# Batch 0's keys in float32 on two hardware queues, with the units of batches 1 to 4 placed anew

## The chip, the cores and the metric

The kernel runs on one core of one Trainium2 chip. The metric is the device time in microseconds (us); three runs of the kernel before gave a median of 245.89 us.

A core has five engines that run beside each other, each through its own instructions in order: TensorE (PE, matrix products), VectorE (DVE), ScalarE (ACT), GpSimd (POOL) and SyncE (SP). Transfers between main memory and on-chip memory (DMA) are issued from SP's, ACT's or POOL's queue. In the profile SP's queue is q1, ACT's is q10 (both "hardware_dynamic") and POOL's is q0 ("software_dynamic").

## What is computed

```python
a = softmax(phi, axis=2)                      # over the sequence; phi is [b, h, s, 32]
k_m = einsum('bhsm,bhsd->bhmd', a, k)         # 32 memory keys a head
v_m = einsum('bhsm,bhsd->bhmd', a, v)         # 32 memory values a head
attn = softmax(q @ k_m.T / sqrt(64), axis=-1)
x = (attn @ v_m)                              # [b, h, s, d] -> [b*s, h*d]
out = ((x @ w_a) * (x @ w_b)) @ w_out
```

There are 8 batches, 8 heads, 576 tokens and a head size of 64, so x has 4608 rows of 512. w_a and w_b are 512 x 1536, w_out is 1536 x 512. All inputs and the output are float32; the kernel computes in float16 with float32 sums.

## The kernel before, in words

The kernel never forms x. For each batch it computes the memory keys and values, folds the values into w_a and w_b (the tile vab), and multiplies vab with the attention weights (the tile A). The products are called "up"; their product by elements goes to the tile ht, and the product of ht with w_out is called "down".

**Units.** The work of a batch ahead of its ups is cut into small pieces (units(b)), which are named by short strings:

- exp0, exp1: exp of half of phi, on ACT (line 194). Phi of batch 0 comes by one DMA, so both wait for all of it.
- ks0, ks1 and vs0, vs1: PE sums of exp times keys and times values, for head groups 0 and 1 (L255), each followed by DVE instructions. ks0 needs keys 0:2, ks1 keys 2:4. For batches 2 and up, kv (L212) does all sums and km (L227, L232, tile rep) takes them to on-chip memory on DVE.
- kt0, kt1, vt0, vt1, or kvt for later batches: PE transposes of those sums, and a DVE copy into kvT (L276, L242).
- qt0 to qt3: DVE transposes of a quarter of q (L203).
- s0, s1 or sc: scores on PE (L292), with four PSUM banks for sc; e0, e1: their exp on ACT (L305).
- den0, den1: sums of E on PE (L314), and the logarithm on ACT (L315).
- nr0, nr1: exp of the negative logarithm on ACT (tile R, L323), and A = E x R (L325), on DVE for batches 0 and 1 and on POOL after.
- v0, v1, v2: PE products that fold a third of w_a and w_b (tile pva, L337); x0a, x0b and so on: the copies to vab, one on ACT and one on DVE (L349). hv and hx are the same for halves of the first third.
- L: load(b + 2), four DMAs on POOL's queue. A number in y3 or y11 means so many down products of the first four row blocks (L389): y1 to y16 need the first third of w_out, y17 to y32 the second, and the rest the last.

A prime in the strings means the batch after, an underscore the batch before.

**Order.** The order is written out by hand. chain(0, ...) and chain(1, ...) run the units of batches 0 and 1 in the order of a string, with f4 for four products of a tile of zeros that keep PE busy. From batch 1 on, ups(...) runs half-steps: four up products (L592), their copy on ACT (a_sb, L600) and the product by elements on DVE (ht, L603); then some of the down products that are due (class Work, L464) and then the next slot of a string. A slot holds units joined by "+"; "-" is empty. The string `second` is used in batch 2 and holds the units of batch 3 and, with a prime, the first ones of batch 4; `every` comes after. The downs of later blocks work on pairs of row blocks with sums of ht (h_sums, L446) that POOL prepares; they are emitted when Work pulls a product that is near them.

**PSUM.** There are eight banks. Banks.take gives the one that was not taken or freed for longest and isn't held, so a product can wait for the ACT or DVE copy that empties its bank.

**Start.** Phi of batch 0 goes by SP's queue and the first half of its keys by ACT's, both in float32. The keys wait in the space of ht and a DVE instruction casts them (L156). The second half of the keys, q, v, the weights and all later batches go by POOL's queue, which casts to float16 on the way (phi stays float32). After the casts DVE fills the tile ones (L160), which two POOL instructions (L161, L163) then change before POOL issues the second third of w_a. 28 fill products run on PE before ks0.

Of the kernel before, what the change touches and what calls it, by code (L numbers as in the profile page):

```python
# [8 lines left out]
F32 = mybir.dt.float32  # L9
# [9 lines left out]
def kernel(  # L19
# [11 lines left out]
    nc = tc.nc  # L31
# [38 lines left out]
    def rows(x, b):  # L70
        return x[b].rearrange("h s d -> (h s d)").rearrange("(c p f) -> p c f", c=NHP, p=P)

    phis, qs, kvs = {}, {}, {}
    kv_sbs = [consts.tile([P, 3, NHP, NI * D], F16, name=f"kv_sb{t}") for t in range(2)]

    def load_phi(b):
        phis[b] = inp.tile([P, NHP, NI * M], F32, name="phi_sb")
        (nc.sync if b == 0 else nc.gpsimd).dma_start(out=phis[b], in_=rows(phi, b))

    def load_k(b, hps=slice(0, NHP)):  # L80
        kvs[b] = kv_sbs[b % 2]
        nc.gpsimd.dma_start(out=kvs[b][:, 0, hps], in_=rows(k, b)[:, hps])

    def load_v(b, hps=slice(0, NHP)):
        nc.gpsimd.dma_start(out=kvs[b][:, 1, hps], in_=rows(v, b)[:, hps])

    def load_q(b, hps=slice(0, NHP)):
        if b not in qs:
            qs[b] = inp.tile([P, NHP, NI * D], F16, name="q_sb")
        nc.gpsimd.dma_start(out=qs[b][:, hps], in_=rows(q, b)[:, hps])  # L90

    def load(b):
        load_phi(b)
        load_k(b)
        load_v(b)
        load_q(b)

    def load_wab(lo, hi):
        nc.gpsimd.dma_start(out=wa_sb[:, :, lo:hi], in_=wa_rows[:, :, lo:hi])
        nc.gpsimd.dma_start(out=wb_sb[:, :, lo:hi], in_=wb_rows[:, :, lo:hi])  # L100
# [4 lines left out]


    ht = consts.tile([P, NFF, 2 * S], F16, name="ht")
    k_f32 = ht[:, 0:2].bitcast(F32)
    nc.scalar.dma_start(out=k_f32, in_=rows(k, 0)[:, 0:2])
    nc.scalar.preload_act_table_set("natural_log_exp_and_others")  # L110
    load_phi(0)
    halves = [slice(0, 2), slice(2, 4)]
    load_q(0, halves[0])
    load_k(0, halves[1])
    load_q(0, halves[1])
    load_v(0)
    kvs[0] = kv_sbs[0]

    warm = consts.tile([P, 512], F16, name="warm")
    nc.vector.memset(warm, 0.0)  # L120
# [26 lines left out]
    def fill(n, cols=512):  # L147

        pw = banks.tile([P, 512], F32, name="pw")
        for _ in range(n):  # L150
            nc.tensor.matmul(pw[:, :cols], warm[:, :P], warm[:, :cols], start=True, stop=True)
# [1 line left out]
    ident = consts.tile([P, P], F16, name="ident")  # L153
    make_identity(nc, ident)
    nc.vector.memset(kv_sbs[0][:, 2], 1.0 / CS)
    nc.vector.tensor_copy(out=kvs[0][:, 0, 0:2], in_=k_f32)  # L156
    load_wab(0, 512)

    ones = consts.tile([P, 4, 32], F16, name="ones")
# [429 lines left out]
    def up_half(b, i, hf, x):  # L589
        ps = banks.tile([P, HALF], F32, name=("pa", "pb")[x])  # L590
        for g in range(2):
            nc.tensor.matmul(ps, vabs[b][x][:, g, P * i:P * (i + 1)], attn[b][:, g, HALF * hf:HALF * (hf + 1)],  # L592
                             start=(g == 0), stop=(g == 1))
        if x == 0:
            if b == 0:
                n = (2 * i + hf) % 20
                a_sbs[b, i, hf] = spare[:, HALF * n:HALF * (n + 1)]
            else:
                a_sbs[b, i, hf] = apool.tile([P, HALF], F16, name="a_sb")
            nc.scalar.copy(out=a_sbs[b, i, hf], in_=ps)  # L600
        else:
            t0 = S * (b % 2) + HALF * hf
            nc.vector.tensor_tensor(out=ht[:, i, t0:t0 + HALF], in0=a_sbs.pop((b, i, hf)), in1=ps, op=ALU.mult)  # L603

    def up(b, i, hfs):
        for hf in hfs:
            up_half(b, i, hf, 0)
        if len(hfs) > 1:
            yield
        for hf in hfs:  # L610
            up_half(b, i, hf, 1)
        yield

    def ups(steps, side=()):

        side = iter(side)
        for step in steps:
            for _ in up(*step):
                work.advance()
                next(side, us[step[0]]["-"])()  # L620
        for f in side:
            work.advance()
            f()
# [5 lines left out]
    def half_steps(b, hf, lo=0):  # L629

        return [(b, i, (hf,)) for i in range(lo, NFF)]
# [10 lines left out]
    def slots(b, names):  # L642

        def both(fs):
            return lambda: [f() for f in fs]
        def unit(n):
            if n == "fin":
                return lambda: work.pull(-work.done % NFF)
            if n == "L":
                return lambda: load(b + 2) if b + 2 < B else None  # L650
            if n[0] == "y":
                return lambda: some(int(n[1:]))
            if n[0] == "d" and n[1:].isdigit():
                return lambda: work.pull(int(n[1:]))
            return us[b + n.endswith("'") - n.endswith("_")][n.rstrip("'_")]

        return [both([unit(n) for n in x.split("+")]) for x in names.split()]
# [3 lines left out]
    def some(n):  # L661
        for _ in range(n):
            next(early, None)

    def chain(b, plan):


        for x in plan.split():
            if x[0] == "f":
                fill(int(x[1:]), 256)  # L670
            elif x[0] == "y":
                some(int(x[1:]))
            elif x[0] in "ab":
                i, _, hf = x[1:].partition(".")
                for h in ([int(hf)] if hf else (0, 1)):
                    up_half(b, int(i), h, "ab".index(x[0]))
            else:
                us[b][x]()
# [3 lines left out]
    chain(0, "v0a x0a f4 a0 a1 v0b x0b f4 b0 b1 a2 b2 v1a x1a a3 b3 a4 a5 v1b x1b a6 a7 b4 b5 v2a x2a b6 b7 a8 a9")  # L682
    load(2)
    chain(0, "v2b x2b a10 a11 b8 b9 b10 b11")
    chain(1, "exp0 exp1 y9 ks0 y3 kt0 qt0 qt1 y1 y3 ks1 qt2 s0 e0 y6 kt1 qt3 den0 y3 s1 nr0 e1 y4 y2 den1 vs0 vs1 vt0 y1 vt1 nr1 hv0a hx0a hv0b y3 hx0b y2")
    load(3)
    sum_weights()
    ups(steps(1, 0, 4), slots(1, "- hv1a+hx1a hv1b+hx1b+y1 - v1a+x1a y3+v1b x1b y3"))
    ups(half_steps(1, 0, 4), slots(1, "- v2a+x2a+v2b+x2b+qt0' - - qt1'+exp0'+qt2' exp1' - kv'+km'+y9"))
    work.plan(S + HALF, 10)  # L690
    ups(half_steps(1, 1, 4), slots(2, "- kvt qt3 sc+e0+e1 - den0+den1 nr0+nr1 v0+x0a x0b - v1+x1b x1a"))
    second = "v2_+x2a_+exp0 x2b_ exp1 - kv+km qt0 qt1 kvt qt2+qt3 sc+e0 e1+v0+x0a den0+x0b v1+x1a nr0+L x1b+exp0' den1 - nr1+v2+x2a - x2b+exp1' - kv'+km' qt0'+qt1' - qt2'+kvt'+qt3'"
    every = "- sc+e0 e1 den0 v0+x0a+x0b - - nr0+exp0' - - v1+x1a qt0' x1b+den1 exp1' - v2+x2a+x2b nr1+qt1' kv'+km' qt2' - qt3' - kvt'+L -"
    last = "sc+e0 - e1 - v0+x0b - x0a den1 - - den0 v1+x1b x1a+nr0 - - - - nr1+v2+x2a - - - - - x2b"
    for b in range(2, B):
# [37 lines left out]
```

The softmax here doesn't subtract the row's maximum and nothing guards it: scores larger than these inputs give would overflow.

## Time and profile before

| | |
|---|---|
| Median of 3 runs | 245.89 us (245.75 to 246.15) |
| The profiled execution | 245.71 us, span 244.0 us |
| Granted PE clock | 0.996 |
| PE, DVE, ACT, POOL busy | 234.6, 166.2, 157.2, 155.6 us |
| Phi of batch 0: issue, landing | 0.81, about 7.0 us |
| First half of batch 0's keys: issue, landing | 0.81, about 6.6 us |
| First key sums (ks0) on PE | 8.81 us |
| Landing of the second third of w_out | 41.06 us |
| First up product of batch 2 | 73.55 us |

The span runs from the first to the last instruction of the program. In the timeline a row is: start, busy time, engine, line, operation, tiles written and read, shapes, count, and in brackets how long the engine stood idle before it and what ended that. PE's matmuls overlap, so a stall can also hide in the length of a row: then the start times tell. POOLq, SPq and ACTq stand for the issue of a DMA.

### The profile page before, as it was taken

The page shows a single profiled execution, that of the slowest core. Times are in us where ns is not written, and L with a number is a line of the kernel's source. Part 1 is how long each engine was busy: PE and PEld are TensorE (multiplying, and loading weights), DVE is VectorE, ACT ScalarE, POOL GpSimd, SP SyncE. Part 2 cuts the span into 40 slices and gives each one's busy share as a digit, 9 for nine tenths or more (in the row PEclk, how much of TensorE's full clock was granted, in tenths as well). Part 3 has the DMA queues.
Part 4 walks back from the last instruction along what each step waited for, and adds up shares of the span by engine and source line. Part 5 has one row for each costly group of instructions (what it writes and reads, how often), then busy time and mean ns, then how long its engine had stood idle before and what let it go on. Part 6 is the DMA issues. An engine that isn't in the chain of part 4 may idle for free.

```text
span 244.0 us, 7661 instructions
## 1 busy us (share of the span) xinstructions
PE 234.6 (96%) x3043; PEld 168.1 (69%) x3043; DVE 166.2 (68%) x401; ACT 157.2 (64%) x406; POOL 155.6 (64%) x130
## 2 busy tenths in 40 slices
PE   7989998999989999999999999999999999999993
PEld 2555654456757857767788777877787878888882
DVE  3446773568949968875994659865996676756642
ACT  2265761679598589578956768587856867565330
POOL 8722263499879629892889759892849177937001
PEclk9999999999999999999999999999999999999998
DMA  6999999999937955973159732696120403042154
GB/s 198 211 207 206 209 254 208 254 224 280 224 89 167 205 110 121 236 128 81 41 146 205 177 86 46 166 203 152 34 58 3 89 0 87 3 89 61 42 128 118
DMA packets 25044, 33.82 MB, mean 139 GB/s; under 512 B 1936, under 2 KB 19472, under 8 KB 25008
## 3 DMA queue, kind: packets, MB, share of 16 engines
q0 software_dynamic: 18288, 22.84, 50.8%
q1 hardware_dynamic: 6208, 9.70, 15.8%
q10 hardware_dynamic: 512, 0.79, 1.0%
q8 instruction: 24, 0.39, 0.7%
q14 instruction: 12, 0.10, 0.1%
HBM read 42.47 MB, written 9.44 MB: 213 GB/s over the span
## 4 chain that ended last, share of the span: by engine, by line
PE 76%; DMA 16%; DVE 3%; ACT 2%; issue 1%; POOL 0%; DVEq 0%
PE pa L592 17%; PE py L464 17%; PE pb L592 16%; PE pv L464 8%; DMA wo_sb<-in_moe_w_out_dram 7%; DMA wa_sb<-in_moe_w_a_dram 6%; PE pva L337 5%; PE px L464 4%; PE po L389 3%; DMA ht<-in_k_dram 2%; PE pkv L212 2%; PE pscore L292 1%; PE pD L314 1%; PE pT L241 1%; ACT E L305 1%
## 5 line engine op out<-in xcount | busy, mean ns | idle before, releaser
L603 DVE TENSOR_TENSOR ht<-a_sb,pb 128x288 f16<-128x288 f16 x168 | 73.2, 448 | 39.4 <-ACT a_sb L600 29.9
L592 PEld LDWEIGHTS <-vab 128*128 128x128 f16 x768 | 71.6, 98 | 27.1 <-issue 9.4
L600 ACT CAST a_sb<-pa 128x288 f16<-128x288 f32 x168 | 66.6, 407 | 26.4 <-PE pa L592 24.3
L592 PE MATMUL pa<-A,vab 128*128 128x288 f16 x384 | 75.7, 287 | 0.4 <-DVE vab L349 0.2
L592 PE MATMUL pb<-A,vab 128*128 128x288 f16 x384 | 75.0, 286 | 0.3 <-ACT vab L349 0.3
L446 POOL TENSOR_TENSOR h_sums<-ht 128x768 f16<-128x768 f16 x28 | 45.9, 1642 | 33.0 <-DVE ht L603 32.4
L464 PEld LDWEIGHTS <-h_sums 128*128 128x128 f16 x384 | 37.3, 98 | 7.0 <-issue 0.5
L349 DVE CAST vab<-pva 128x512 f16<-128x512 f32 (+1 forms) x50 | 32.3, 663 | 3.3 <-PE pva L337 2.6
L349 ACT CAST vab<-pva 128x512 f16<-128x512 f32 (+1 forms) x50 | 27.9, 581 | 9.3 <-PE pva L337 9.1
L464 PEld LDWEIGHTS <-ht 128*128 128x128 f16 x288 | 28.1, 98 | 5.7 <-issue 0.4
L464 PE MATMUL py<-w_sums,h_sums 128*128 128x256 f16 x192 | 30.4, 272 | 0.0
L446 POOL TENSOR_TENSOR h_sums<-ht,h_sums 128x768 f16<-128x768 f16 x14 | 23.0, 1642 | 1.0
L446 POOL TENSOR_TENSOR h_sums<-h_sums,ht 128x768 f16<-128x768 f16 x14 | 23.0, 1642 | 0.9
L325 POOL TENSOR_TENSOR A<-E,R 128x576 f16<-128x576 f16 x12 | 15.3, 1278 | 8.8 <-ACT R L323 8.6
L305 ACT ACTIVATE E<-pscore 128x288 f16<-128x288 f32 x32 | 11.4, 417 | 14.5 <-PE pscore L292 14.5
L464 PE MATMUL pv<-w_sums,h_sums 128*128 128x256 f16 x96 | 16.2, 273 | 0.0
L464 PE MATMUL py<-wo_sb,ht 128*128 128x256 f16 x96 | 16.0, 273 | 0.0
L471 ACT ACTIVATE u<-py 128x256 f32<-128x256 f32 x32 | 12.6, 393 | 5.2 <-PE py L464 4.9
L203 DVE STREAM_TRANSPOSE qT<-q_sb 128x288 f32<-128x288 f32 x32 | 14.3, 461 | 2.3 <-DMA q_sb<-in_q_dram 2.3
L464 PE MATMUL py<-w_sums,ht 128*128 128x256 f16 x96 | 15.5, 272 | 0.1
L464 PE MATMUL px<-wo_sb,ht 128*128 128x256 f16 x96 | 15.4, 273 | 0.0
L194 ACT ACTIVATE exp_sb<-phi_sb 128x576 f16<-128x576 f32 x16 | 11.0, 698 | 5.3 <-DMA phi_sb<-in_phi_dram 5.3
(65 smaller groups left out, 274.5 us busy)
## 6 DMA issues: line engine op xcount, KB each, us to landing
out_dram<-o_sb SPq DMA_DIRECT2D x68, 128.0 KB, 2.4
kv_sb<-in_v_dram POOLq DMA_DIRECT2D x7, 576.0 KB, 11.4
phi_sb<-in_phi_dram POOLq DMA_DIRECT2D x7, 576.0 KB, 5.2
kv_sb<-in_k_dram POOLq DMA_DIRECT2D x7, 576.0 KB, 9.0
q_sb<-in_q_dram POOLq DMA_DIRECT2D x6, 576.0 KB, 13.6
wa_sb<-in_moe_w_a_dram POOLq DMA_DIRECT2D x3, 512.0 KB, 14.4
wb_sb<-in_moe_w_b_dram POOLq DMA_DIRECT2D x3, 512.0 KB, 16.2
wo_sb<-in_moe_w_out_dram POOLq DMA_DIRECT2D x3, 512.0 KB, 18.1
```

The source lines that it names most:

```text
L194: nc.scalar.activation(out=t["exp"][:, 2 * z:2 * z + 2, :, :], in_=phis[b][:, 2 * z:2 * z + 2, :].rearrange("p c (i m) -> p c i m", m=M), ...
L203: nc.vector.transpose(out=t["qT"][:, hp, :].bitcast(F32), in_=qs[b][:, hp, :].bitcast(F32))
L305: nc.scalar.activation(out=Ev[:, g, :, z, :], in_=pss, func=AF.Exp, scale=1.0 / (8.0 * CS))
L325: engine.tensor_tensor(out=attn[b][:, g, sl], in0=t["E"][:, g, sl], in1=t["R", g][:, sl], op=ALU.mult)
L337: nc.tensor.matmul(t["pva", lo, z][g][0][32 * j:32 * j + 32, 0:hi - lo], t["kvT"][64 * r:64 * r + 64, 4 + g, M * j:M * j + M], w_sbs[z][64 ...
L349: engine_copy(out=vabs[b][z][:, g, lo:hi], in_=pva[:, 0:hi - lo])
L446: engine.tensor_tensor(out=out, in0=in0, in1=in1, op=op)
L464: nc.tensor.matmul(po, lhs[:, i], rhs[:, i], start=first and i == 0, stop=i == KH - 1, skip_group_check=not first)
L471: nc.scalar.mul(out=x, in_=po, mul=scale)
L592: nc.tensor.matmul(ps, vabs[b][x][:, g, P * i:P * (i + 1)], attn[b][:, g, HALF * hf:HALF * (hf + 1)], start=(g == 0), stop=(g == 1))
L600: nc.scalar.copy(out=a_sbs[b, i, hf], in_=ps)
L603: nc.vector.tensor_tensor(out=ht[:, i, t0:t0 + HALF], in0=a_sbs.pop((b, i, hf)), in1=ps, op=ALU.mult)
```

## The change

Five things are changed.

1. Both halves of batch 0's keys are loaded in float32, the first on SP's queue and the second on ACT's. The second half leaves POOL's queue.
2. Phi of batch 0 is issued on SP's queue behind the first key half.
3. DVE casts the two halves in two instructions, both ahead of the tile ones.
4. In chain(1) the units and the early downs have another order: twelve downs before ks0, ks1 directly behind it, kt1 before the six downs that need the second third of w_out, qt0 and qt1 apart, vs and vt spread.
5. In the slots of batch 2 (in the second half of batch 1) qt3 comes first, nr0 goes with den0 and den1, and nr1 one slot later. In `second`, kvt and nr0 of batch 3 come one slot earlier, den1 three slots later (the 19th), nr1 four later (the 22nd); of batch 4, exp1 comes three slots earlier, and qt0 and qt1 come in the 19th and 22nd slots instead of together in the 23rd.

```diff
-    k_f32 = ht[:, 0:2].bitcast(F32)
-    nc.scalar.dma_start(out=k_f32, in_=rows(k, 0)[:, 0:2])
+    k_f32 = ht[:, 0:4].bitcast(F32)
+    halves = [slice(0, 2), slice(2, 4)]
+    for engine, x in zip((nc.sync, nc.scalar), halves):
+        engine.dma_start(out=k_f32[:, x], in_=rows(k, 0)[:, x])
     nc.scalar.preload_act_table_set("natural_log_exp_and_others")
     load_phi(0)
-    halves = [slice(0, 2), slice(2, 4)]
-    load_q(0, halves[0])
-    load_k(0, halves[1])
-    load_q(0, halves[1])
+    kvs[0] = kv_sbs[0]
+    for x in halves:
+        load_q(0, x)
     load_v(0)
-    kvs[0] = kv_sbs[0]
...
-    nc.vector.tensor_copy(out=kvs[0][:, 0, 0:2], in_=k_f32)
+    for x in halves:
+        nc.vector.tensor_copy(out=kvs[0][:, 0, x], in_=k_f32[:, x])
...
-    chain(1, "exp0 exp1 y9 ks0 y3 kt0 qt0 qt1 y1 y3 ks1 qt2 s0 e0 y6 kt1 qt3 den0 y3 s1 nr0 e1 y4 y2 den1 vs0 vs1 vt0 y1 vt1 nr1 hv0a hx0a hv0b y3 hx0b y2")
+    chain(1, "exp0 y1 exp1 y11 ks0 ks1 y1 qt0 y3 kt0 qt1 s0 e0 kt1 y6 qt2 qt3 den0 y3 s1 nr0 y4 vs0 e1 vs1 den1 y1 vt1 y2 vt0 nr1 hv0a hx0a hv0b y2 hx0b y3")
...
-    ups(half_steps(1, 1, 4), slots(2, "- kvt qt3 sc+e0+e1 - den0+den1 nr0+nr1 v0+x0a x0b - v1+x1b x1a"))
-    second = "v2_+x2a_+exp0 x2b_ exp1 - kv+km qt0 qt1 kvt qt2+qt3 sc+e0 e1+v0+x0a den0+x0b v1+x1a nr0+L x1b+exp0' den1 - nr1+v2+x2a - x2b+exp1' - kv'+km' qt0'+qt1' - qt2'+kvt'+qt3'"
+    ups(half_steps(1, 1, 4), slots(2, "qt3 kvt - sc+e0+e1 - den0+den1+nr0 - v0+nr1+x0a x0b - v1+x1b x1a"))
+    second = "v2_+x2a_+exp0 x2b_ exp1 - kv+km qt0 kvt+qt1 - qt2+qt3 sc+e0 e1+v0+x0a den0+x0b nr0+v1+x1a L x1b+exp0' - exp1' v2+x2a den1+qt0' x2b - nr1+qt1'+kv'+km' - - qt2'+kvt'+qt3'"
```

## The prediction

> **What bounds the kernel now.** I read the page first, then the DMA queues in short windows, the chain of waits, and the timelines of each engine around every place where TensorE (PE) stops. Page, busy times and slices:
>
> ```profile
> span 244.0 us, 7661 instructions
> PE 234.6 (96%) x3043; PEld 168.1 (69%) x3043; DVE 166.2 (68%) x401; ACT 157.2 (64%) x406; POOL 155.6 (64%) x130
> ...
> DMA  6999999999937955973159732696120403042154
> ```
>
> PE is busy nearly all the time, so only its stalls and the warm-up fills can be won. DMA is full in the ten slices after the first (6 to 67 us). DMA queues in three windows (2 to 3, 4 to 5, 7 to 8 us; packets, MB written, share):
>
> ```profile
> q1 hardware_dynamic: 109, 0.13, 66.2%
> q10 hardware_dynamic: 11, 0.03, 14.7%
> ...
> q10 hardware_dynamic: 118, 0.27, 68.6%
> q1 hardware_dynamic: 118, 0.14, 37.6%
> ...
> q0 software_dynamic: 187, 0.20, 119.7%
> ```
>
> The casting queue q0 writes 0.20 MB a us in half precision, so it reads 0.41; the two hardware queues together moved 0.41 from 4 us on. Either way the core reads about 410 GB/s: a byte of float32 costs the same on each queue. Only 2 to 4 us is below it (151 and 271 GB/s). PE's timeline:
>
> ```profile
> 37.23 0.68 PE L255 MATMUL pk<-kv_sb,exp_sb 64*32 64x128 f16 x36 [0.80 <-DMA kv_sb<-in_k_dram]
> ...
> 41.10 1.45 PE L389 MATMUL po<-wo_sb,ht 128*128 128x512 f16 x6 [0.24 <-DMA wo_sb<-in_moe_w_out_dram]
> ...
> 85.65 0.47 PE L292 MATMUL pscore<-qT,kvT 32*32 32x288 f16 x32
> ...
> 103.54 1.15 PE L292 MATMUL pscore<-qT,kvT 32*32 32x288 f16 x32
> ```
>
> Until 41 us PE follows the loads (keys of batch 1, then the second third of w_out). The chain says the same: DMA 16%, and one step from w_out's issue at 22.95 to its landing at 41.06. Later stalls are short: the same 32 score matmuls take 0.47 us at 85.65 and 1.15 at 103.54. POOL's and ACT's timelines, for the steps that move:
>
> ```profile
> 89.11 1.64 POOL L446 TENSOR_TENSOR h_sums<-ht 128x768 f16<-128x768 f16 x1 [5.86 <-DVE ht L603]
> 91.58 1.28 POOL L325 TENSOR_TENSOR A<-E,R 128x576 f16<-128x576 f16 x1 [0.84 <-ACT R L323]
> ...
> 99.20 1.27 POOL L325 TENSOR_TENSOR A<-E,R 128x576 f16<-128x576 f16 x1
> 100.43 1.65 POOL L446 TENSOR_TENSOR h_sums<-ht 128x768 f16<-128x768 f16 x1
> ...
> 70.19 1.36 ACT L323 ACTIVATE R<-L 128x576 f16<-128x576 f32 x2
> ```
>
> **What the Trainium skill says.** DMA: Bandwidth & Descriptors, section "Issuing engines are not separate DMA queues": all issuers' transfers run on the same 16 engines, and more issuers save issue time alone. The trace agrees: 410 GB/s read on both kinds. Same page, "Queues, rings and completion order": each DMA engine takes the queues in turn by packets. Between 98 and 98.5 us q0 moved 45 packets and q1 35, which fits. Same page, "SWDGE vs HWDGE vs iDMA": a cast is possible only from GpSimd; so keys on the other queues stay float32, and VectorE (DVE) must cast them.
>
> **The change, part by part.**
>
> *Start, queues.* POOL loses one DMA issue (0.73 us at 2.18), so its later issues come 0.73 earlier; they only join a queue that is full. SP gains one issue (0.45) ahead of phi's. ACT issues the other half instead. DVE gains a second cast of 0.76; the casts are followed by the memset of ones and POOL's two selects (7.65 and 8.03), ahead of POOL's next weight issue. Keys should land at about 5.7 instead of 6.64, since they no longer share with phi; casts to 7.2, so that place does not move. If keys land as late as now, POOL's issue is 0.8 late, hidden by 9 us of loads already queued.
>
> Bytes: 0.59 MB leave q0 and come to hardware; at 410 GB/s both are 1.44 us, net nothing. What can be won is the slope at the start. At 2 to 3 us q1 moved 109 packets of 1152 bytes, each some 95 ns; key packets have 2304 bytes at 93 to 100 ns. At the same packet rate 2 to 4 us moves up to 0.25 MB more: 0.25/0.41 = 0.6 us earlier for everything behind. If bytes set the slope it is nothing. I take 0.35, ends 0 and 0.65.
>
> *Phi behind a key half.* Keys (1.18 MB) need until about 5.3. Then phi's 512 packets share with q0, which began at 5.25 to 5.5. Packet for packet (about 55 and 98 ns on 16 engines: 103 pairs a us), with some 150 sent before, 362/103 = 3.5 us: landing at about 9.4 (7.0 now; ends 8.2 and 10.5). The first exp (0.65) and ks0 then start at 10.1 instead of 8.81: 1.35 late. Queued behind ks0 on PE is all of chain(0). Of the delay 1.0 vanishes in the stall before vs0 (15.75, waits for v), so chain(0) is some 0.35 late from 18 to 34 us.
>
> *Units of batch 1.* Three more of the 0.216 us down matmuls stand ahead of ks0 (12 instead of 9) and fill its 0.97 stall (start to start). ks1 and kt1 (0.3) move ahead of the wait for w_out. PE so reaches that wait at 40.86 - 0.97 + 0.3 = 40.2, plus 0.35 late, still before 41.06 - 0.35 = 40.7. The load stays last; delay covered. After it, s1 waits for q (42.5), vs1 for v (45.4), y33 on for the last w_out (47.9), all earlier by the 0.35; kt1 done beforehand and the gaps at 46.61 and 47.67 (0.27 and 0.29) partly filled win 0.1 more, since w_out at 47.9 comes next. At 49 us: 0.45 early (ends -0.1 and 0.85).
>
> *Units of batch 2 (61 to 74).* qt3 goes two steps earlier, off DVE's place beside the scores: scores end 0.15 earlier. nr0 goes ahead of one a_sb copy and one u copy on ACT: R0 starts at 69.7, POOL's first A (1.28) ends at 71.7; but R1 (0.68) now stands behind the last a_sb copy and ends at 72.0 instead of 71.55, and the copies behind it are 0.35 later. Waiting behind R0 is the a_sb copy that frees v0's third bank (PE stalls some 0.4 there, and recovers it at v1). A1 ends at 72.1 + 1.28 = 73.4 instead of 73.58, which is what the first up matmul of batch 2 waits for. 0.15 won (ends -0.2 and 0.4).
>
> *Units of batch 3 (76 to 102).* kvt one step earlier: PE comes to it at 81.16, DVE's last rep ends at 81.33: 0.1 lost (0 to 0.2). nr0 one step earlier: R0 ends at 90.6 and POOL's A at 92.0 instead of 92.86; the four DMA issues of the load, then three h_sums, stand before A1. In program order a third h_sums (1.65) now precedes A1, as nr1 is four steps later: 92.0 + 3.05 + 3 x 1.65 + gaps = 100.1, and A1 ends at 101.4. Batch 3's first up is at 101.61: just covered. I put 0.1 (0 to 0.6, the latter if POOL does not start earlier). The later exp and den1 fall into ACT's dense stretch and cost nothing that PE waits for: those copies have over two steps.
>
> *Units of batch 4 (99 to 105).* qt0' and qt1' leave the stretch between rep's end (101.13) and the scores: DVE saves two transposes of 0.46 there, in which it has no gap; they go to 95 to 99, where it stood idle 0.67 and 0.85. kvT and qT are ready by 103.25 and the scores need 0.47 instead of 1.15: 0.5 won (ends 0.3 and 0.85).
>
> From 106 on PE is full and the order is unchanged: what is won stays. Sum: 0.45 + 0.15 - 0.1 - 0.1 + 0.5 = 0.9 us. The profiled execution took 245.71 (span 244.0 and 1.7 around it): 244.8. The median shown is 245.89, 0.18 above: 245.0. A measurement tells about 0.2% (0.5 us) from no change.
>
> **Rivals.** (a) More, by the good ends: 0.65 + 0.1 + 0.4 - 0.1 - 0.1 + 0.85 = 1.8, so 244.1. For: packets' equal duration; against: ACT is full there. (b) No difference: the slope is set by bytes or latency, POOL's A1 is late by 0.4 and eats the gain at the scores: 0.1 + 0.15 - 0.1 - 0.4 + 0.5 = 0.25, so 245.6. For: 410 GB/s binds both queues, and A1's cover is 0.2. (c) Slower: phi starves. It decides from a landing at 9.9, where the lateness (landing + 0.75 - 8.81 = 1.86) exceeds the 1.0 at vs0 and the 0.86 at w_out. If q0 gets two packets to phi's one (362 x 0.25/16 = 5.7 us) phi lands at 11.6: 1.7 beyond, of which the waits of s1, vs1 and hv0a take back some 0.65; the 0.45 is lost, 0.45 of the later gains stays: 1.05 - 0.45 = +0.6, 246.5. Against: at 98 us the two took nearly equal turns, and at 5.5 to 6.5 phi still got through. That the change does not do what it says has no room: the instruction order of each engine moves as the diff says.
>
> **How the numbers follow.** Forecast 0.45, (a) 0.12, (b) 0.29, (c) 0.14. Range: the forecast's own 244.2 to 245.5; to leave out no more than two in ten it takes in (b) and most of (c), and (a): 244.1 to 246.4. Faster by over 0.2% (under 245.4) 0.57, within 0.30, slower 0.13.
>
> **What would show it.** Key packets of 2304 bytes on both queues from 2 us with over 200 GB/s at 2 to 3; phi landing 8.2 to 10.5, ks0 at about 10; the stall before vs0 shrunk; w_out landing near 40.7 with PE waiting for it; batch 2's first up 0.6 earlier than 73.55; the scores at 103 in about half a us; A1 ending before batch 3's first up. Wrong if loads land no earlier, phi lands after 9.9, or POOL's A1 holds up PE at 101.

## The result and the profile after

The changed kernel takes 260.11 us (median of 4 runs, 259.31 to 260.96) where the kernel before, run beside it, takes 245.84 (4 runs, 245.75 to 246.15). The ratio is 1.0579, with a 95% interval of 1.0541 to 1.0616: slower by 14 us, and far outside the range that was forecast. The profiled execution took 259.78 us, with a span of 257.8 and a mean granted clock of 0.967. Two kernels among the experiments below gave their times in two groups 15 us apart; for these the single times are told.

The page of the kernel after, busy times, slices and the end of the chain of waits (line numbers are one higher than before's from the casts on):

```profile
span 257.8 us, 7661 instructions
PE 235.8 (91%) x3043; PEld 168.6 (65%) x3043; DVE 179.4 (70%) x402; ACT 157.5 (61%) x406; POOL 154.7 (60%) x129
...
PE   8599999802999999999999999999999999999993
...
POOL 6623264596008892898379985987494639749001
PEclk9979999965899999999999999999999999999999
...
PE 83%; DVE 7%; DMA 4%; ACT 3%; issue 1%; SPq 0%; DVEq 0%
```

PE has 1.2 us more work but 13.8 us more span. Its row has a hole in the ninth and tenth slices (51 to 64 us), and a smaller one in the second (from 8.2 to 11.2 us, where it waits for phi of batch 0). DVE's busy time grew by 13.2 us with one instruction more, a cast of 0.75: something else on DVE became long. The chain puts 7% of the span on DVE. The groups of the page say which one, and PE's waits (in all, times, longest) say what it held up:

```profile
L326 DVE TENSOR_TENSOR A<-E,R 128x576 f16<-128x576 f16 x4 | 14.4, 3604 | 4.5 <-ACT R L324 4.5
```
```profile
PE pa L593 <- DVE vab L350: 11.8, 2, 11.7
PE pk L256 <- ACT exp_sb L195: 3.0, 1, 3.0
```

Four products A = E x R on DVE have a mean of 3.6 us, though the first of batch 1 takes 0.46 (below). The timelines of DVE, then of POOL, then of PE in that stretch:

```profile
46.29 0.46 DVE L326 TENSOR_TENSOR A<-E,R 128x576 f16<-128x576 f16 x1 [1.93 <-ACT R L324]
...
49.50 13.04 DVE L326 TENSOR_TENSOR A<-E,R 128x576 f16<-128x576 f16 x1
62.46 0.74 DVE L350 CAST vab<-pva 128x256 f16<-128x256 f32 x2
```
```profile
48.69 0.75 POOL L90 DMA_DIRECT2D q_sb<-in_q_dram  x1
49.45 3.25 POOL L432 TENSOR_TENSOR w_sums<-wo_sb 128x768 f16<-128x768 f16 x2
...
59.01 3.21 POOL L432 TENSOR_TENSOR w_sums<-wo_sb,w_sums 128x768 f16<-128x768 f16 x2
```
```profile
50.99 0.29 PE L593 MATMUL pa<-A,vab 128*128 128x288 f16 x1
62.93 0.90 PE L593 MATMUL pa<-A,vab 128*128 128x288 f16 x3 [11.66 <-DVE vab L350]
```

The first A of batch 1 takes 0.46 us. The second (unit nr1 of chain(1)) starts at 49.50, 0.05 us after POOL has begun the eight sums of the halves of w_out (`sum_weights`, called right behind `load(3)`), and ends at 62.54, 0.3 us behind the last of the eight. DVE works in order, so the copies of vab behind it wait too, and with them PE: 11.66 us. In the kernel before the same two instructions (DVE, then POOL) stood the other way round, A first with 1.2 us to spare:

```profile
47.53 0.45 DVE L325 TENSOR_TENSOR A<-E,R 128x576 f16<-128x576 f16 x1
```
```profile
48.42 0.74 POOL L90 DMA_DIRECT2D q_sb<-in_q_dram  x1 [0.82 <-DVE A L325]
49.17 3.25 POOL L431 TENSOR_TENSOR w_sums<-wo_sb 128x768 f16<-128x768 f16 x2
```

The same places in both traces, before and after, give where the 14 us arose:

| Place | before | after | later by |
|---|---|---|---|
| ks0 of batch 0 | 8.81 | 11.18 | 2.4 |
| first folded matmul (v0a) | 17.79 | 20.40 | 2.6 |
| first early down in chain(1) | 34.33 | 36.92 | 2.6 |
| first up of batch 1 | 49.10 | 50.99 | 1.9 |
| end of batch 1's second A | 47.98 | 62.54 | 14.6 |
| fifth half-step of batch 1 | 58.72 | 74.12 | 15.4 |
| first up of batch 2 | 73.55 | 88.27 | 14.7 |
| scores of batch 4 | 103.54 | 118.08 | 14.5 |
| last rows | | | 14.0 |

So in this execution some 1.9 us are the start's, 13.5 the blocked A's, and the slots won 1.4 back.

### The profile page after: what moved, and what is told of

The parts are those of the page before. It is cut to its first block, busy times and chain, and to the rows that moved or that the text cites. A ratio compares the mean times of both kernels' runs of the same rounds, so it can differ in the third digit from the quotient of the medians.

```text
span 257.8 us, 7661 instructions
## 1 busy us (share of the span) xinstructions
PE 235.8 (91%) x3043; PEld 168.6 (65%) x3043; DVE 179.4 (70%) x402; ACT 157.5 (61%) x406; POOL 154.7 (60%) x129
## 4 chain that ended last, share of the span: by engine, by line
PE 83%; DVE 7%; DMA 4%; ACT 3%; issue 1%; SPq 0%; DVEq 0%
PE pa L593 19%; PE pb L593 18%; PE py L465 16%; PE pv L465 8%; DVE A L326 5%; PE pva L338 5%; PE po L390 4%; PE px L465 4%; DMA phi_sb<-in_phi_dram 4%; PE pkv L213 2%; PE pscore L293 2%; PE pk L256 1%; PE pD L315 1%; PE pw L151 1%; ACT E L306 1%
## 5 line engine op out<-in xcount | busy, mean ns | idle before, releaser
L593 PE MATMUL pa<-A,vab 128*128 128x288 f16 x384 | 76.8, 290 | 12.1 <-DVE vab L350 11.8
L326 DVE TENSOR_TENSOR A<-E,R 128x576 f16<-128x576 f16 x4 | 14.4, 3604 | 4.5 <-ACT R L324 4.5
## 6 DMA issues: line engine op xcount, KB each, us to landing
q_sb<-in_q_dram POOLq DMA_DIRECT2D x6, 576.0 KB, 13.5
```

The lines of the kernel that those rows point to most:

```text
L326: engine.tensor_tensor(out=attn[b][:, g, sl], in0=t["E"][:, g, sl], in1=t["R", g][:, sl], op=ALU.mult)
```

## The experiments

Theory 1 is that a DVE product with two inputs in SBUF waits while POOL reads SBUF, here for the whole burst of eight sums, and that the change let A slip behind the burst's start; part of it (1b) is that DVE is not let in between two of POOL's instructions. The rivals are that the order alone does it (the new chain(1) makes a wait of its own, whatever POOL does), or the late phi alone. Beside them stands the question of what the start and the slots are worth. Ratios are to the kernel before on the same chip.

The edits of start_only, start_chain, chain_slots, after_guard, after_gap, after_memsets and phi_first are shown against the kernel after, those of chain_only, slots_only and late_nr1 against the kernel before, start_guard's against start_only and start_fill's against start_guard; three dots stand for what is left out.

**start_only**: the new loads and casts, with the old chain(1) and slots.

```diff
-    chain(1, "exp0 y1 exp1 y11 ks0 ks1 y1 ... y2 vt0 nr1 hv0a hx0a hv0b y2 hx0b y3")
+    chain(1, "exp0 exp1 y9 ks0 y3 kt0 ... y1 vt1 nr1 hv0a hx0a hv0b y3 hx0b y2")
...
```

> The kernel before with the new start alone (both key halves in float32, phi behind the first; two casts). Theory 1 (collision): the 13 us are lost because batch 1's second product A = E x R on DVE becomes ready 0.05 us after POOL has begun its eight sums of w_out, and DVE then waits for all eight; this takes the late start and the new order of batch 1 together. With the old order nr1 stands ahead of what releases POOL, so A (0.46 us) begins about 0.5 us before the sums: no block, ks0 2.4 late, first up of batch 1 some 1.9 late, total about 247.7. Theory 2 (phi): the late start alone carries the loss: 258 or more. Theory 3 (the order of batch 1 alone): 245.8.

Measured: 260.57, 262.56, 246.15 and 261.79 us, beside 245.52 for the kernel before. The old order of the units is blocked too: by the times in three executions of four, and the profiled one (260.57) is among them. So the new order is not needed for it. The miss: theory 1 had put A in time here. DVE's and POOL's timelines of the profiled execution:

```profile
48.32 13.90 DVE L326 TENSOR_TENSOR A<-E,R 128x576 f16<-128x576 f16 x1
```
```profile
48.38 0.75 POOL L90 DMA_DIRECT2D q_sb<-in_q_dram  x1
49.13 3.25 POOL L432 TENSOR_TENSOR w_sums<-wo_sb 128x768 f16<-128x768 f16 x2
```

By the trace A starts 0.8 us ahead of the first sum, and 0.06 ahead of a DMA issue of POOL behind which the sums stand queued; it ends at 62.22, again 0.3 us behind the last sum. Starts on POOL are rough; how A was caught there stays open (more at start_guard).

**chain_only**: the new chain(1) alone.

```diff
-    chain(1, "exp0 exp1 y9 ks0 y3 kt0 ...")
+    chain(1, "exp0 y1 exp1 y11 ks0 ks1 y1 ...")
```

> The kernel before with the new order of batch 1's units alone. Theory 1 (collision): A is ready about 1.9 us after vs1, near 47.9, while POOL's sums are held until 49.2 by the issue of the load of batch 3 ahead of them: no block, A takes 0.46 us, total 245.2 to 246.2. Theory 2: 245.8 as well. Theory 3 (the order alone): A takes 13 us, 258 or more.

Measured: 245.65 us, ratio 1.0005 (0.9996 to 1.0013). A runs from 47.53 for 0.46 us, the sums start at 49.10. The order alone does nothing; that rival falls.

**slots_only**: the new slots of batch 2 and the new `second` alone.

```diff
-    ups(half_steps(1, 1, 4), slots(2, "- kvt qt3 sc+e0+e1 - den0+den1 nr0+nr1 v0+x0a x0b - v1+x1b x1a"))
+    ups(half_steps(1, 1, 4), slots(2, "qt3 kvt - sc+e0+e1 - den0+den1+nr0 - v0+nr1+x0a x0b - v1+x1b x1a"))
...
```

> The kernel before with the new slots of batches 2 to 4 alone. If what the changed kernel won between 74 and 130 us (its lag to the kernel before fell from 15.4 to 14.0) is the slots' own: 245.84 - 1.4 = 244.4. If it only took back lag from the late start and the slow clock: 245.8. The prediction had 0.15 - 0.1 - 0.1 + 0.5 = 0.45 for them: 245.4.

Measured: 244.14 us, ratio 0.9949 (0.9935 to 0.9964). This is better than both kernels, and the lowest median of all; chain_slots (below) is as low within the intervals.

**start_chain**: the new start and the new chain(1), with the old slots.

```diff
-    ups(half_steps(1, 1, 4), slots(2, "qt3 kvt - ..."))
+    ups(half_steps(1, 1, 4), slots(2, "- kvt qt3 ..."))
...
```

> New start and new order of batch 1, old slots of batches 2 to 4. Theory 1: the collision needs these two and nothing else: A of batch 1 takes 13 us on DVE, total 260.1 + 1.4 = 261.5. If the new slots had a part in it: about 248.

Measured: 260.99 us, ratio 1.0635 (1.0613 to 1.0656); A takes 13.10 us. Start and chain together hold the whole loss.

**chain_slots**: the old start, with all the rest of the change.

```diff
-    k_f32 = ht[:, 0:4].bitcast(F32)
+    k_f32 = ht[:, 0:2].bitcast(F32)
...
```

> Old start, new order of batch 1 and new slots of batches 2 to 4. Theory 1 (collision of A with POOL's sums, which needs PE late): no block, A of batch 1 takes 0.46 us, and the two parts add: 245.65 - 1.4 = 244.2. If the new order and slots need the new start to win: about 245.5.

Measured: 244.4 us, ratio 0.9955 (0.9942 to 0.9969), as slots_only within the intervals. Without the new start the change is a gain.

**after_guard**: the kernel after, in which POOL reads one column of the finished A ahead of the sums, so that these cannot start before it.

```diff
     load(3)
+    seen = small.tile([P, 1], F16, name="seen")
+    nc.gpsimd.tensor_copy(out=seen, in_=attn[1][:, 1, 0:1])
     sum_weights()
```

> The changed kernel with one POOL instruction more ahead of the eight sums of w_out: a copy of one column of batch 1's second A, so that POOL waits for that A. Theory 1: A takes some 0.5 us instead of 13, POOL's sums begin some 0.6 later, and what is left is the late start (1.9 at the first up of batch 1) less the 1.4 of the slots: 246.0 to 246.5. If something else held DVE for 13 us: 259 or more.

Measured: 245.58 us, ratio 1.0009 (0.9992 to 1.0025). Not one of twelve runs was blocked (the longest took 247.38). One instruction of 0.19 us takes back some 14 us. DVE's and POOL's timelines:

```profile
48.49 0.46 DVE L326 TENSOR_TENSOR A<-E,R 128x576 f16<-128x576 f16 x1
```
```profile
48.02 0.74 POOL L90 DMA_DIRECT2D q_sb<-in_q_dram  x1 [0.34 <-DVE kvT L277]
49.02 0.19 POOL L689 COPY seen<-A 128x1 f16<-128x1 f16 x1 [0.25 <-DVE A L326]
49.16 3.24 POOL L432 TENSOR_TENSOR w_sums<-wo_sb 128x768 f16<-128x768 f16 x2
```

A begins inside the DMA issue and takes its 0.46 us: the issue itself does not block. The sums start no later than in the kernel before, so the guard costs nothing that shows. Other work of DVE is not held by the sums: beside them in the kernel before, from 49.2 to 62 us, fifteen ht products (one input from SBUF, one from PSUM) take 443 ns each, against 448 over the whole span. The product that waits has both inputs in SBUF.

**after_gap**: the kernel after with a short memset of POOL behind each sum, a break in which POOL reads nothing.

```diff
+        gap = small.tile([P, 128], F16, name="gap")
...
                 nc.gpsimd.tensor_tensor(out=out[:, sl], in0=in0[:, sl], in1=in1[:, sl], op=ALU.subtract)
+                nc.gpsimd.memset(gap, 0.0)
```

> The changed kernel with a POOL memset of 128 columns (it reads nothing; some 0.25 us) behind each of the eight sums. Theory 1a: DVE waits only while POOL reads, and gets in at the first break: A ends behind the first sum, 1.7 to 2 us after its start, total 248 to 249. Theory 1b: a waiting DVE instruction is let in only once POOL's queue has nothing ready: A takes 13 + 2 = 15 us, total about 262.

Measured: 260.87 us, ratio 1.0616 (1.0595 to 1.0637). Seven breaks, and DVE is let into none of them; A ends at 63.31, 0.3 us behind the last sum, which is now later. The breaks are short: by the rows the memset overlaps the end of the sum before it, and some 0.1 us lie between two sums. A longer break was not tried.

```profile
49.25 14.06 DVE L326 TENSOR_TENSOR A<-E,R 128x576 f16<-128x576 f16 x1
```
```profile
49.20 1.66 POOL L433 TENSOR_TENSOR w_sums<-wo_sb 128x768 f16<-128x768 f16 x1
50.79 0.22 POOL L434 MEMSET gap<- 128x128 f16 x1
50.96 1.64 POOL L433 TENSOR_TENSOR w_sums<-wo_sb 128x768 f16<-128x768 f16 x1
```

**late_nr1**: the kernel before with nr1 at the end of chain(1), and nothing of the change.

```diff
-    chain(1, "... vt0 y1 vt1 nr1 hv0a hx0a hv0b y3 hx0b y2")
+    chain(1, "... vt0 y1 vt1 hv0a hx0a hv0b y3 hx0b y2 nr1")
```

> The kernel before (old start, old orders) with nr1 of batch 1 moved to the end of its chain, 8 down products and 32 fold products later, so that A becomes ready after POOL's sums began at 49.2. Theory 1: A takes 12 to 13 us, total about 259, with no late start and none of the change's orders. If the block needs the float32 keys or phi's place: 246 to 247.

Measured: 260.93 us, ratio 1.0618 (1.0597 to 1.064). A starts at 50.28, behind the sums' start at 49.18, and takes 11.99 us, again to 0.3 us behind the end of the sums. The collision can be had from the kernel before, by A's place alone, with phi in time. DVE's and POOL's timelines:

```profile
50.28 11.99 DVE L325 TENSOR_TENSOR A<-E,R 128x576 f16<-128x576 f16 x1 [1.47 <-ACT R L323]
```
```profile
48.42 0.74 POOL L90 DMA_DIRECT2D q_sb<-in_q_dram  x1 [0.83 <-DMA wo_sb<-in_moe_w_out_dram]
49.18 3.24 POOL L431 TENSOR_TENSOR w_sums<-wo_sb 128x768 f16<-128x768 f16 x2
```

**start_guard**: start_only with the guard, so that the start is priced without the block.

```diff
-    sum_weights()
+    seen = small.tile([P, 1], F16, name="seen")
+    nc.gpsimd.tensor_copy(out=seen, in_=attn[1][:, 1, 0:1])
+    sum_weights()
```

> The new start alone (start_only), with the POOL copy that makes the eight sums wait for batch 1's second A. Theory 1: every run is without the block; ks0 some 1.8 late, first up of batch 1 0.8 to 1.0 late, total 246.3 to 246.6. This is also the start's own price. If POOL's issue of the last load (0.75 us ahead of the sums) blocks DVE, A still takes 0.8 us or more.

Measured: 246.71 us (five runs, 246.28 to 247.05), ratio 1.0045 (1.0029 to 1.0062). Not one run was blocked. The new start by itself loses 1.3 us. A (48.73, for 0.45 us) starts here as in start_only 0.06 us ahead of the same DMA issue of POOL (48.79), and is not held. What differs is that the sums behind the issue now wait for A, which points to them, and not to the issue, as what held it in start_only. The late phi by itself, the other rival, is worth 1.3 us and not 14.

**start_fill**: start_guard with 32 instead of 12 of the small filler matmuls ahead of batch 0's ks0, so that PE does not stand idle while it waits for phi.

```diff
-    chain(0, "exp0 exp1 qt0 qt1 f12 ks0 f4 ...")
+    chain(0, "exp0 exp1 qt0 qt1 f32 ks0 f4 ...")
```

> start_guard with 20 more fill products ahead of ks0 (32 instead of 12), so that PE does not idle for 2 to 3 us while phi is late. If the idle time lowers the granted clock afterwards (0.5 to 0.8 between 11 and 16 us in the changed kernel) and that costs a part of the lateness: the clock stays near 1.0, first fold product 0.3 to 0.9 us earlier than in start_guard, total about 246.0. If phi's landing alone sets it: as start_guard.

Measured: 245.54 us, ratio 1.0007 (0.9999 to 1.0016): 1.2 us less than start_guard. ks0 runs as late as there (10.95 and 10.96), but from 11.2 to 16 PE has its full clock. Windows of start_guard, then of start_fill (length, then busy time and count of PE, PEld, DVE, ACT, POOL; then granted clock, DMA share, GB/s):

```profile
11.20:13.00 1.80, 1.80 (x46) 0.84 (x34) 0.75 (x3) 0.28 (x1) 0.62 (x1) 0.71 1.21 206
13.00:16.00 3.00, 2.85 (x65) 1.49 (x65) 0.88 (x4) 0.71 (x2) 0.76 (x1) 0.61 1.26 211
```
```profile
11.20:13.00 1.80, 1.75 (x62) 1.02 (x54) 0.74 (x3) 0.00 (x0) 0.64 (x1) 1.00 1.23 209
13.00:16.00 3.00, 2.82 (x85) 1.47 (x72) 1.49 (x5) 1.42 (x4) 0.76 (x1) 1.00 1.23 206
```

In the same 4.8 us PE does 111 matmuls against 147. At batch 1's first up start_guard is 1.20 us behind the kernel before, start_fill 0.08. So phi's lateness is absorbed, as the prediction had it; the slow clock behind the idle stretch was not.

**after_memsets**: the kernel after with each of the eight sums replaced by a memset of the same tile. The sums are left out, so that what is computed from them is not.

```diff
-                nc.gpsimd.tensor_tensor(out=out[:, sl], in0=in0[:, sl], in1=in1[:, sl], op=ALU.subtract)
+                nc.gpsimd.memset(out[:, sl], 0.0)
```

> The changed kernel with the eight sums of w_out on POOL replaced by eight memsets of the same tiles, which write as much and read nothing (the sums, and so the outputs that use them, are left out). Theory 1 with a shared read port: A on DVE takes 0.46 us beside them, total 245 to 246.5. If any running POOL instruction blocks DVE: A takes about 5 us (eight memsets of some 0.7 us), total about 251.

Measured: 245.99 us, ratio 1.0024 (1.0011 to 1.0036). A starts at 49.28, inside a row of memsets that began at 49.19 and last 5.5 us, and takes 0.46: POOL's writes do not hold it up, its reads do. DVE's and POOL's timelines:

```profile
49.28 0.46 DVE L326 TENSOR_TENSOR A<-E,R 128x576 f16<-128x576 f16 x1
```
```profile
49.19 5.52 POOL L432 MEMSET w_sums<- 128x768 f16 x8
```

**phi_first**: the new slots, the old chain(1), and a start with both key halves in float32, but phi issued first.

```diff
-    for engine, x in zip((nc.sync, nc.scalar), halves):
+    load_phi(0)
+    for engine, x in zip((nc.scalar, nc.sync), halves):
         engine.dma_start(out=k_f32[:, x], in_=rows(k, 0)[:, x])
     nc.scalar.preload_act_table_set("natural_log_exp_and_others")
-    load_phi(0)
...
```

> New slots of batches 2 to 4, old order of batch 1, and the new start with phi ahead: phi and then the second key half on SP's queue, the first half on ACT's. ks0 returns to 8.8 (phi no longer behind a key half) and the loads keep the 0.5 us that the changed kernel gained. If that 0.5 reaches PE: 243.7. If PE's own order sets the pace from 18 us on: as slots_only, 244.1.

Measured: of twelve runs seven took 244.61 to 245.74 (ratio of these 0.9986, 0.9975 to 0.9997) and five 260.13 to 261.24. A miss. In the profiled execution, one of the five, ks0 starts at 7.62, but then the second key half is late (DVE's cast of it starts at 9.69, and what PE needs next comes behind it on DVE), PE stands idle 2.86 us and works at half the clock from 11.2 to 18 us; v0a comes 2.94 us later than before. A starts at 49.30, ahead of the first sum (50.11) as in start_only, and takes 13.89 us. In both orders tried, the transfer put last makes PE wait once, and in these profiles pay in clock.

## Why the prediction was wrong

*The step that failed* is "Units of batch 1". It followed what PE waits for in this stretch (w_out, q, v), put the whole stretch down as "0.45 early", and never set nr1's product beside POOL's sums: it has no term for that wait, which measured 13.5 us. For a wait on a semaphore its way of looking is enough. Here there is no semaphore between the two: they share a way into SBUF. The Trainium skill says so, in SBUF — State Buffer, section "Who interferes with whom": a DVE instruction with two SBUF inputs contends with a GpSimd instruction that reads SBUF, not with one that only writes it, and "Issue order, not op shape, decides who blocks." The runs agree that reads block (13.04 us) and writes do not (0.46 us), and after_guard turns the order and gets 0.46 back. That the two share a read path is the page's account; the runs show only who waits for whom. In two points they differ. The page, where it speaks of DVE's two-port modes, gives the shared pair to the first for the whole instruction, which here would be 1.63 us; measured is the whole burst of eight, with short breaks as without. And in start_only and phi_first the A whose record starts first is the one that waits.

*Why the order turned* is a margin that no row names. Sums and A hang on the same PE work: `load(3)`'s v waits for PE's last read of batch 1's keys and values, q's issue follows (0.75 us), then the sums. A waits for den1 on PE, two activations on ACT, and DVE. In the kernel before, q and the sums also come behind the last third of w_out (47.9 us), and that held them back while A ran: 1.2 us between A's end and the first sum. The row of that kernel puts the wait of q's issue down to A itself; but in late_nr1, where A comes last, the issue starts at the same 48.42, there put down to w_out. When PE is 2 us late that load no longer sets the sums' start (q's issue starts at 48.69, right behind v's), and in the new chain nr1's place leaves the two in a dead heat: 49.45 and 49.50. So the new order alone is harmless (chain_only), the new start alone is caught in some executions (start_only), and the two together were caught in all eight runs that had them with the sums and no guard (after, start_chain, after_gap).

*Start, queues*: right in size. Key packets of 2304 bytes filled the slope (272 GB/s against 173 from 2.5 to 3 us, with about as many packets as before). From 2 to 3 us it was 187 and not the 200 that was named, since the half us before that had fewer packets (22 against 56); from 3 to 4 it was 376 against 271. In the two us that is 0.14 MB more, or 0.34 us at 410 GB/s. Queues in that window, packets, MB and share, kernel after:

```profile
q1 hardware_dynamic: 52, 0.12, 67.4%
q10 hardware_dynamic: 7, 0.02, 12.9%
```

The keys landed at 5.7 and 6.1 (issue 0.81 and about 4.9 and 5.3 us more), and the second third of w_out at 40.5, 0.5 earlier than before where 0.35 was put.

*Phi behind a key half*: the mechanism was right, the size at its upper end. q0 and q1 do take turns, as from 6.5 to 7 us in the kernel after:

```profile
q0 software_dynamic: 55, 0.06, 72.9%
q1 hardware_dynamic: 58, 0.07, 45.6%
```

But phi landed at 10.4 in this profile, not 9.4, past the point of 9.9 that rival (c) gave; in the other profiles of this start it landed from 9.7 to 10.2. The pairs were as fast as put (some 110 a us from 6.5 to 8). But the 150 packets taken as sent when q0 begins, at 5.5, were sent only by 6.0, since the keys ran until 5.5; and at the end the turns are no longer even: from 8.5 us on, in each half us, phi got 46, 39, 14 and 2 packets and q0 62, 70, 88 and 99. What (c) expected to follow, lateness beyond the covers, was still absorbed (start_fill: ks0 2.1 late, batch 1's first up 0.08). What followed instead appears in no part of the prediction: a clock of 0.78 and 0.56 after PE's idle stretch. Windows of the kernel after:

```profile
11.20:13.00 1.80, 1.80 (x50) 1.07 (x50) 0.53 (x3) 0.50 (x1) 0.56 (x1) 0.78 1.21 206
13.00:16.00 3.00, 3.00 (x65) 1.48 (x64) 0.86 (x4) 0.55 (x2) 0.76 (x1) 0.56 1.24 207
```

The Trainium skill, TensorE: Matmul & The Clock Gate, section "HAM oscillation — how this bites in real kernels", warns of PE idle gaps over some 3.4 us; here 2.96 us sufficed, and in start_only's profile 2.68 (clock 0.53 from 11.2 to 13 us). It does not follow in every execution: in the profiles of after_guard and start_chain, with the same start, PE stood idle only 1.69 and 1.86 us ahead of ks0, and the clock stayed at 1.00. "The load stays last; delay covered" failed in this execution: PE came to the second third of w_out at 43.2, 2.7 us after the load; in start_fill, with the full clock, it came at 41.2.

*The slots*: right in sign, too small. By slots_only's trace beside before's, "units of batch 2" won 0.7 where 0.15 was put: R1 began at 70.75 and A1 ended at 72.92, half a us ahead of the forecast 73.4. PE loses half a us at v0's second fold, as was put (0.89 us for eight pva matmuls, 0.40 before), but gains at the next two, where 0.90 before became 0.41 and a stall of 0.19 is gone. "Units of batch 3" cost nothing (two terms of 0.1 were put; POOL's A1 ended at 100.37 and held nobody up). "Units of batch 4" won 0.7 where 0.5 was put: the scores start 0.2 earlier beyond the lead of before and last half a us less. PE's timeline, slots_only:

```profile
102.54 0.64 PE L292 MATMUL pscore<-qT,kvT 32*32 32x288 f16 x32
```

That is 1.4 from the slots instead of 0.45, which is the 245.52 less 244.14 us of the medians. In the kernel after the gain is there too (15.4 late at 74 us, 14.0 at the end), hidden by a loss ten times as large.

## What to carry to other kernels

When a change moves an engine's work by even a us, look for what runs beside it on engines that share something without a semaphore: list the stretches in which POOL reads SBUF for long, and each DVE instruction with two SBUF inputs near their start or inside them, and ask by how much the order stands. If the margin is luck, fix it with a dependency: a read of one column by POOL cost 0.19 us and saved some 14. And a transfer made later can cost more than the wait if PE stands idle over it (2.7 us and more in these profiles), because the clock falls; fillers that go on until the data is there took that back here (246.71 to 245.54).

## What the runs showed of the hardware

A DVE product of 0.46 us waited 13.04 us for eight sums of POOL back to back (1.63 us each), 14.06 us with memsets of 0.2 us between them, 11.99 us when it came 1.1 us after their start (these times include its own run), and not at all beside 5.5 us of memsets or while POOL issued DMAs (start_guard: A from 48.73 to 49.18, issues from 48.05 to 49.54). That it waits for the whole queue of reads is measured; why breaks of some 0.1 us between two reads do not let it in is not. Nor is settled why, in start_only, an A whose record starts 0.8 us ahead of the first sum was caught: the records on POOL are rough, and its DMA issue stood between, behind which the sums were queued. In start_guard the same place ahead of the issue did no harm once the sums waited. That batch 1's A be given to POOL, as for the later batches, was not tried.

A PE stall of 11.66 us was followed by half the clock for another 3.6 us, and one of 2.96 us by a clock of 0.78 from 11.2 to 13 us and 0.56 from 13 to 16. In five profiles with an idle stretch of 2.68 to 3.20 us ahead of ks0 the clock fell to a half soon after (after, start_only, start_guard, after_gap, after_memsets); in two with 1.69 and 1.86 us it did not (after_guard, start_chain). Where between the two the limit lies, and what else it hangs on, these runs do not show.
